# The first row stage of a Fourier and mixer kernel: second fold moved into the matmuls, small steps moved between engines, order of loads and scales changed

## The chip, the cores and the metric

The kernel runs on one core of a Trainium2 chip. The core's engines each work through a queue of their own in order: TensorE (PE in the profile; PEld is its loading of stationary operands), VectorE (DVE), ScalarE (ACT), GpSimd (POOL), and SyncE (SP), which here only issues DMAs. The metric is the device time of one execution in microseconds (us); lower is better.

## What is computed

Two operations are applied in turn, twice. The first adds to x the inverse transform of a filtered two-dimensional Fourier transform of its layernorm; the second is a token-mixing MLP. x has 2048 rows of 640 numbers, in float32.

```python
def _A_ref(x, w_r, w_i):
    X = rfft2(x)
    X = X * (w_r + 1j * w_i)
    return irfft2(X, s=(2048, 640))

x = x + _A_ref(_layernorm(x), w_r, w_i)
x = x + mixer_mlp(_layernorm(x), w1, b1, w2, b2)
x = x + _A_ref(_layernorm(x), w_r, w_i)
x = x + mixer_mlp(_layernorm(x), w1, b1, w2, b2)
```

## The kernel before

The 2048 rows lie in 16 tiles of 128 partitions by 640 columns, called row tiles 0 to 15 here. The whole program is written by hand as straight-line code; inside the stages spoken of here each engine executes its instructions in the order in which they are written (`self.pin`).

**The first row stage** (in `run`, a loop over steps i) takes each row tile through these steps, one step of the loop apart or so:

- SP loads the tile `xt` and, every fourth tile, a transform table `tM`. Further loads bring the sixteen filter tiles `w`.
- DVE takes the row statistics (`stats1`: two BATCH_NORM_STATS2, tile `st`; `stats2`: one BATCH_NORM_AGGREGATE, tile `mv`).
- ACT makes `nm` = -mean and `v` = variance + eps; POOL makes `r` = v to the power -1/2 and `nb` = nm times r; ACT makes the normalized tile `z`.
- First fold (`a0_fold1`): symmetric columns are added and subtracted by POOL, two TENSOR_TENSOR of 320 columns and a COPY of two columns, into `eo` (two buffers). POOL also sets two columns of `z` to zero.
- Second fold (`a0_fold2`): DVE adds and subtracts the halves of `eo` into `f` (two buffers): two instructions of 256 columns, two of 64 and a COPY.
- PE (`a0_s1f`): first `FILL` = 7 matmuls on constant data, which are no part of the result, then five float32 products of 128 columns each of `f` with the tile's table, into one of four PSUM tiles (`ps`).
- ACT and DVE evict the sums as a float16 pair: `s1h` (ACT) and `s1l` (DVE).

Beside these runs a scan: ACT squares every filter tile `w` with an accumulator (`jw`), from which a power-of-two scale `sx` for the filtered spectrum is found (`scale_x`); `scale_b` does the like for a bias. After the scans the first five tiles of `w` are fetched again (`self.wx`, `wfetch`) for the next stage.

**The next stage** (`a1`) follows a list of steps, `STEPS`. `d0`, `d1`, ... are PE's products along the columns; `d0` needs `s1h` and `s1l` of all sixteen row tiles. `ea1` to `ev9` are parts of `scale_b` and `scale_x`. From `d2` on, one operand, `stk`, is a part of `s1h` and `s1l` that was written to DRAM (`rest`) and read back in another layout. `sA0`, `sB0` and so on are PE's next products, `ph`, `pl`, `ta`, `tb` evictions and filtering by ACT and DVE.

Of the kernel before, what the change touches and what calls it, by code (L numbers as in the profile page):

```python
# [24 lines left out]
NW = 5  # L25
NSTK = 3
WARM = 4
FILL = 7
STEPS = '''
    ea1 ev1 ep8 ep1 ev8 ev2 d1@1 ep9 ev9 sA0@2 ph1 pl1 sB0 d2@3 sA1@0 d3@1 ph2&1 tb0 ta0 pl2 sa0 ph3 sB1 sb0 sA2@2 d4@3  # L30
    tb1 xh0&2 pl3 sB2 sA3@1 ta1 ph4&3 tb2 ta2 xl0 d6@0 sa1 sb1 ph6 sB3 xh1 d5@2 pl4 sa2 ta3 pl6 sb2 sA4@3 ph5 tb3 ul0&4
# [61 lines left out]
class Layers:  # L93
# [160 lines left out]
    def scan_x(self, pool, g):  # L254

        w = self.t(pool, [128, 2, NL], F32, "w", 3)
        self.nc.sync.dma_start(w, self.A["w"][g])
        junk = self.t(pool, [128, 2, NL], BF16, "jw", 1)
        return lambda: self.T.activation(junk, w, AF.Square, accum_out=self.xq[:, g:g + 1])

    def scale_x(self, pool, ps):

        V, mm = self.V, self.PE.matmul
        mm(ps[:NG, 0, 322:450], self.xq, self.eye, start=True, stop=True)
        yield
        m = pool.tile([NG, 1], F32, name="xm")
        V.tensor_reduce(m, ps[:NG, 0, 322:450], op=ALU.max, axis=mybir.AxisListType.X)
        b = pool.tile([NG, 128], F32, name="xb")
        V.tensor_copy(b, m.to_broadcast([NG, 128]))
        yield  # L270
        mm(ps[:, 1, 322:322 + NG], b, self.eye[:NG, :NG], start=True, stop=True)
        yield
        q = pool.tile([128, NG], F32, name="xqq")
        V.tensor_scalar(q, ps[:, 1, 322:322 + NG], SMALL, XS ** -2, op0=ALU.max, op1=ALU.mult)
        i = self.t(self.base, [128, NG], F32, f"qi{NG}", 1)
        a, b = i.bitcast(I32), self.sx.bitcast(I32)
        V.tensor_scalar(a, q.bitcast(I32), EXPO, 1, op0=ALU.bitwise_xor, op1=ALU.logical_shift_right)
        V.tensor_scalar(b, a, EXPO, None, op0=ALU.bitwise_and)
        V.tensor_scalar(self.sx, self.sx, 2.0 ** 63, None, op0=ALU.mult)
        yield  # L280
        V.tensor_scalar(a, b, EXPO, None, op0=ALU.bitwise_xor)
        V.tensor_scalar(q, i, EC * 0.5 / TS, None, op0=ALU.mult)
        of = pool.tile([128, NG], F32, name="xof")
        V.tensor_reduce(of, self.eye.rearrange("p (g a) -> p g a", g=NG), op=ALU.add, axis=mybir.AxisListType.X)
        V.tensor_tensor(of, of, q, op=ALU.mult)
        V.tensor_reduce(self.cxe, of, op=ALU.add, axis=mybir.AxisListType.X)
        yield
# [32 lines left out]
    def a0_open(self, first=False):  # L320
# [12 lines left out]
        if first:  # L333
            self.tM = [p.tile([128, 4, 128], F32, name=f"tM{q}_{self.n}") for q in range(4)]
        else:
            self.tM = [p.tile([128, 4, 2, 128], F16, name=f"tM{q}_{self.n}") for q in range(4)]
            self.tM32 = p.tile([128, 128], F32, name=f"tMf{self.n}")
# [37 lines left out]
    def a0_fold2(self, eo, between=lambda: None, gp=False):  # L375
# [6 lines left out]
        ea, eb = eb[:, :, 0:160], eb[:, :, 161:321]  # L382
        V.tensor_tensor(f4[:, 0::3], ea[:, :, :128], eb[:, :, :128], op=ALU.add)
        V.tensor_tensor(f5[:, 0::3], ea[:, :, 128:], eb[:, :, 128:], op=ALU.add)
        between()
        W.tensor_tensor(f4[:, 1:3], ea[:, :, :128], eb[:, :, :128], op=ALU.subtract)
        W.tensor_tensor(f5[:, 1:3], ea[:, :, 128:], eb[:, :, 128:], op=ALU.subtract)
# [19 lines left out]

    def a0_s1f(self, j, f):
        ps = self.big().rearrange("p a b -> p (a b)")
        for _ in range(FILL if j else 4 * FILL):  # L410
            self.PE.matmul(ps[:, :512], self.fill[:, :128], self.fill[:, 128:], start=True, stop=True)
        for t in range(5):
            c = slice(t * 128, t * 128 + 128)
            self.PE.matmul(ps[:, c], f[:, c], self.tM[j // 4][:, j % 4], start=True, stop=True)
        return ps[:, :D].rearrange("p (a h b) -> p a h b", h=2, b=4)
# [9 lines left out]
    def a0_tail(self, j, z, st, pend):  # L425
# [26 lines left out]
        for i, (c, w) in enumerate(((slice(0, 128), 512), (slice(128, 160), 128))):  # L452
            f = self.t(p, [128, w], F32, f"ft{i}", 1)
            f4 = f.rearrange("p (c b) -> p c b", c=4)
            V.tensor_tensor(f4[:, 0::3], ea[:, :, c], eb[:, :, c], op=ALU.add)
            V.tensor_tensor(f4[:, 1:3], ea[:, :, c], eb[:, :, c], op=ALU.subtract)
            if i:
# [25 lines left out]
    def a1(self, first):  # L483
# [268 lines left out]
        def scale(op):  # L752

            n = int(op[2:])
            if n > 7:
                if n == 8 and op[1] == "p":
                    made["x"] = self.scale_x(p, slots[3])
                next(made["x"])
            elif op == "ea1":
                made["b"] = self.scale_b(at=lambda: slots[3][:, 1, 400:401])  # L760
                next(made["b"])
            elif op in ("ev1", "ep1", "ev2"):
                next(made["b"])
            elif op in ("ea2", "ea3"):
# [1235 lines left out]
    def run(self):  # L2000
# [10 lines left out]
        self.eye = self.base.tile([128, 128], F32, name="eye")  # L2011
        scans = []
        x, st, z, eo, f, pv, vs, nms = ({} for _ in range(8))

        def load(i):
            if i < NJ:
                x[i] = self.t(self.pT, [128, D], F32, "xt", 6)
                self.lastld = nc.sync.dma_start(x[i], self.xs[0][i])
                if i % 4 == 0:
                    nc.sync.dma_start(self.tM[i // 4], A["tM32"][:, i:i + 4])  # L2020

        for i in range(3):
            load(i)
        self.pin = True
        for i in range(NJ + 6):
            load(i + 3)
            has = [0 <= i - k < NJ for k in range(7)]
            if has[6]:
                self.a0_s1h(i - 6, pv[i - 6], 1.0)
            if has[1]:  # L2030
                vs[i - 1] = self.t(self.pT, [128, 1], F32, "v", 2)
                nms[i - 1] = self.t(self.pT, [128, 1], F32, "nm", 2)
                self.T.activation(nms[i - 1], st[i - 1][:, 0:1], AF.Copy, scale=-1.0)
                self.T.activation(vs[i - 1], st[i - 1][:, 1:2], AF.Identity, bias=self.eps)
            if has[5]:
                pv[i - 5] = self.a0_s1f(i - 5, f.pop(i - 5))
            if has[3]:
                eo[i - 3] = self.a0_fold1(z.pop(i - 3))
            if has[2]:
                z[i - 2] = self.a0_norm(x.pop(i - 2), *st.pop(i - 2))  # L2040
            if has[0]:
                s1 = self.stats1(self.pT, x[i])
            if has[4]:
                s2 = []
                f[i - 4] = self.a0_fold2(eo.pop(i - 4), lambda: has[0] and s2.append(self.stats2(self.pT, s1)))
            elif has[0]:
                s2 = [self.stats2(self.pT, s1)]
            if has[0]:
                st[i] = s2[0]
            for k in () if i == 18 else (i - 7, i - 6) if i == 19 else (i - 6,):  # L2050
                if 0 <= k < NJ:
                    self.a0_s1l(k, pv.pop(k), 1.0)
            if has[1]:
                mv = st[i - 1]
                r = self.t(self.pT, [128, 1], F32, "r", 2)
                self.G.tensor_tensor(r, vs.pop(i - 1), self.mh, op=ALU.pow)
                b = self.t(self.pT, [128, 1], F32, "nb", 2)
                self.G.tensor_tensor(b, nms.pop(i - 1), r, op=ALU.mult)
                st[i - 1] = r, b
            if 4 <= i < NG + 4:  # L2060
                scans.append(self.scan_x(pw, i - 4))
            for _ in range(2 if i in (18, 19) else 1):
                if i >= 6 and scans:
                    scans.pop(0)()
# [232 lines left out]
```

## Time and profile before

| | us |
|---|---|
| median of 3 runs | 957.31 (956.43 to 957.54) |
| the profiled execution, its own time | 956.78 |
| its span, first to last instruction | 955.0 |

The profile is of that one execution; the 1.78 us by which its time exceeds its span lie around the instructions. Nearly all vector, scalar and GpSimd instructions go through one helper and carry its line, L85, so that groups are told apart by their tiles: `f<-eo` is an instruction that reads `eo` and writes `f`. "x2 [0.17 <-DVE f]" says that the row holds two instructions, that the engine was idle for 0.17 us before the first, and that an instruction of DVE on `f` ended the wait. In a row that groups several instructions, the duration runs from the first start to the last end. The row stage takes about the first 61 us of the span.

### The profile page before, as it was taken

To read this page: it belongs to the slowest core of one execution; us is meant where nothing else is said; L and a number is where in the kernel's file an instruction comes from. 1 tells how busy PE (TensorE), PEld (TensorE's weight loads), DVE (VectorE), ACT (ScalarE), POOL (GpSimd) and SP (SyncE) were. 2 spreads that over 40 slices of the span, in tenths; PEclk is the share of its full clock that TensorE was granted. 3 is DMA by queue.
4 is the path that set the end of the run, shared out by engine and by line. 5 is a ranking of instruction groups with operands and counts; after the bars stand their busy time and mean duration, and the time that the engine had idled before them with its cause. 6 is when DMAs were issued, how large, how long until landed. Compare 5 with 4: busy or idle time off the path is not lost.

```text
span 955.0 us, 22612 instructions
## 1 busy us (share of the span) xinstructions
PE 939.0 (98%) x9086; PEld 686.8 (72%) x9086; DVE 767.9 (80%) x1411; ACT 572.6 (60%) x889; POOL 301.1 (32%) x483
## 2 busy tenths in 40 slices
PE   8999999999999999999999999999999999999998
PEld 4667777767777777777777777777777777777776
DVE  7979999999888968877775898889745456998885
ACT  5857969895767665555543476884533335455542
POOL 6939968311111113332223596770000000000000
PEclk9999999999999999999999999999999999999999
DMA  7956367743886756755333655874554446555411
GB/s 252 310 174 193 103 205 239 244 177 138 302 309 233 254 197 232 259 187 178 115 118 119 174 167 168 264 242 157 159 170 158 150 129 238 190 185 186 142 55 48
DMA packets 69537, 179.50 MB, mean 188 GB/s; under 512 B 7836, under 2 KB 16312, under 8 KB 69432
## 3 DMA queue, kind: packets, MB, share of 16 engines
q1 hardware_dynamic: 62760, 153.94, 50.1%
q0 software_dynamic: 6672, 24.12, 6.6%
q8 instruction: 71, 1.16, 0.5%
q14 instruction: 34, 0.28, 0.1%
HBM read 130.45 MB, written 47.58 MB: 186 GB/s over the span
## 4 chain that ended last, share of the span: by engine, by line
PE 81%; DVE 9%; DMA 3%; ACT 2%; issue 2%; POOL 2%; SPq 1%; POOLq 0%; ACTq 0%; DVEq 0%
PE ps L85 81%; DVE st L85 1%; DMA raw<-w 1%; DVE f L85 1%; DVE s1l L85 1%; DVE Yl L85 1%; DVE xt L85 1%; DVE hl L85 1%; DVE hf L85 1%; DVE hlb L85 1%; POOL eo L85 1%; DMA xt<-x 1%; POOL xt L85 0%; DMA rest<-s1l 0%; ACT eh L85 0%
## 5 line engine op out<-in xcount | busy, mean ns | idle before, releaser
L85 PEld LDWEIGHTS <-wh 128*128 128x128 f16 x2290 | 221.9, 98 | 85.9 <-ACT wh L85 0.4
L85 PE MATMUL ps<-u,wh 128*128 128x320 f16 x1234 | 227.2, 299 | 0.0
L85 PEld LDWEIGHTS <-wl 128*128 128x128 f16 x1617 | 157.8, 98 | 62.1 <-issue 0.7
L85 PE MATMUL ps<-u,wl 128*128 128x320 f16 x817 | 180.7, 299 | 0.0
L85 PEld LDWEIGHTS <-wo 128*128 128x128 f16 x917 | 89.7, 98 | 34.8
L85 POOL TENSOR_TENSOR r<-v,mh 128x1 f32<-128x1 f32 x64 | 38.5, 601 | 123.3 <-DVE nm L85 113.7
L85 PE MATMUL ps<-tDi,Yh 128*128 128x322 f16 x320 | 69.9, 300 | 0.9 <-ACT Yh L85 0.8
L85 ACT ACTIVATE junk<-raw 128x896 bf16<-128x896 f32 (+1 forms) x60 | 59.5, 992 | 9.2 <-DMA raw<-w 8.1
L85 DVE SCALAR_TENSOR_TENSOR wl<-raw,s,wh 128x896 f16<-128x896 f32 (+2 forms) x43 | 55.7, 1304 | 11.3 <-ACT wh L85 11.3
L85 POOL TENSOR_TENSOR eo<-z 128x320 f32<-128x320 f32 x60 | 57.2, 974 | 18.6 <-ACT z L85 14.5
L85 POOL TENSOR_TENSOR xt<-xt,ec 128x320 f32<-128x320 f32 x64 | 53.3, 854 | 25.9 <-DVE xt L85 25.8
L85 DVE BATCH_NORM_STATS2 st<-xt 128x6 f32<-128x320 f32 x126 | 55.3, 480 | 4.9 <-DMA xt<-x 4.1
L85 PE MATMUL ps<-u,wo 128*128 128x320 f16 x413 | 57.9, 299 | 0.0
L85 PE MATMUL ps<-tDi,Yl 128*128 128x322 f16 x192 | 54.2, 299 | 0.1
L85 ACT ACTIVATE wh<-raw,s 128x896 f16<-128x896 f32 (+2 forms) x46 | 45.1, 988 | 6.1 <-PE ps L85 6.1
L85 POOL TENSOR_TENSOR xl<-ta,xh 128x642 f16<-128x642 f32 (+2 forms) x34 | 45.6, 1345 | 5.2 <-ACT xh L85 4.2
L85 DVE SCALAR_TENSOR_TENSOR u<-f,su,u 128x1280 f16<-128x1280 f32 (+2 forms) x26 | 25.5, 997 | 25.2 <-ACT u L85 25.1
L85 PE MATMUL ps<-hhb,wh 128*128 128x320 f16 x256 | 43.4, 299 | 0.0
L85 DVE TENSOR_TENSOR f<-eo 128x256 f32<-128x256 f32 x124 | 39.0, 367 | 5.0 <-POOL eo L85 3.5
L85 ACT ACTIVATE z<-xt,nb,r 128x640 f32<-128x640 f32 x31 | 28.5, 919 | 23.8 <-POOL z L85 15.9
L85 PE MATMUL ps<-tD,s1h 128*64 128x160 f16 (+1 forms) x576 | 39.3, 236 | 1.3 <-DVE Yl L85 0.7
L85 PEld LDWEIGHTS <-Yh 128*128 128x128 f16 x320 | 28.7, 97 | 14.4 <-ACT Yh L85 1.2
(262 smaller groups left out, 2217.3 us busy)
## 6 DMA issues: line engine op xcount, KB each, us to landing
xt<-x SPq DMA_DIRECT2D x79, 320.0 KB, 3.2
raw<-w SPq DMA_DIRECT2D x32, 512.0 KB, 7.0
w<-w SPq DMA_DIRECT2D x48, 321.0 KB, 3.4
x<-xt SPq DMA_DIRECT2D x47, 320.0 KB, 2.8
raw<-w SPq DMA_DIRECT2D x32, 448.0 KB, 5.2
raw<-w2z SPq DMA_DIRECT2D x32, 448.0 KB, 4.2
out<-xt SPq DMA_DIRECT2D x15, 320.0 KB, 2.2
w1S<-wl POOLq DMA_DIRECT2D x9, 512.0 KB, 6.1
```

Source lines behind the costliest of these rows:

```text
L85: i = f(*a, **k)
```

## The change

- In the first row stage the second fold is no longer done by DVE for the 128 main columns of each half. `eo` itself is the stationary operand, and PE multiplies it with the table and then with the table followed by its negative, summing in PSUM: four float32 products of 256 columns each take the place of four of 128. Only the last 32 columns of each half are still folded by DVE (`a0_rest`, tile `fr`). ACT makes the negative tables, one instruction per four row tiles.
- `eo` has three buffers, and its two odd columns are copied by DVE. The zero columns of `z` are set once.
- DVE adds eps to the variance; POOL's `nb` comes from one TENSOR_SCALAR on `mv`; ACT's `nm` and `v` go.
- The loads start with row tiles 0 and 1, then the table, then row tile 2. The filter tiles are scanned in the order 5 to 15, 0 to 4, and the last five stay for the next stage. The other tables load at step 13 in place of 8.
- `scale_b` and all of `scale_x` but its end run inside the loop and right behind it; their steps leave the head of `STEPS`.
- `FILL` is 1. The loop has 21 steps in place of 22.
- The order of the column groups changes, so `a0_fold2`, `a0_tail` and `dstage`, which the second layer uses too, index them in another order.

```diff
-FILL = 7
+FILL = 1
...
-    ea1 ev1 ep8 ep1 ev8 ev2 d1@1 ep9 ev9 sA0@2 ph1 pl1 sB0 d2@3 sA1@0 d3@1 ph2&1 tb0 ta0 pl2 sa0 ph3 sB1 sb0 sA2@2 d4@3
+    d1@1 sA0@2 ph1 pl1 sB0 d2@3 sA1@0 d3@1 ph2&1 tb0 ta0 pl2 sa0 ph3 sB1 sb0 sA2@2 d4@3
...
     def scan_x(self, pool, g):
 
-        w = self.t(pool, [128, 2, NL], F32, "w", 3)
-        self.nc.sync.dma_start(w, self.A["w"][g])
+        if g < NW:
+            w = self.wx[g] = self.wfetch(g)
+        else:
+            w = self.t(pool, [128, 2, NL], F32, "w", 4)
+            self.nc.sync.dma_start(w, self.A["w"][g])
         junk = self.t(pool, [128, 2, NL], BF16, "jw", 1)
...
         return ps[:, :D].rearrange("p (a h b) -> p a h b", h=2, b=4)
 
-    def a0_s1f(self, j, f):
+    def a0_fold0(self, z):
+
+        G, V = self.G, self.V
+        eo = self.t(self.pT, [128, 646], F32, "eo", 3)
+        v2 = lambda a, o, w: a[:, o:o + 2 * w].rearrange("p (a b) -> p a b", a=2)[:, :, 0:160]
+        za, zb = v2(z, 1, 161), v2(z, 321, 160)
+        V.tensor_copy(eo[:, 0:162:161], z[:, 0:162:161])
+        G.tensor_tensor(v2(eo, 1, 161), za, zb, op=ALU.add)
+        self.lastpool = G.tensor_tensor(v2(eo, 322, 161), za, zb, op=ALU.subtract)
+        return eo
+
+    def a0_rest(self, eo):
+
+        V = self.V
+        f = self.t(self.pT, [128, 128], F32, "fr", 2)
+        f4 = f.rearrange("p (c b) -> p c b", c=4)
+        eb = eo[:, 0:644].rearrange("p (a b) -> p a b", a=2)
+        ea, eb = eb[:, :, 128:160], eb[:, :, 289:321]
+        V.tensor_tensor(f4[:, 0::3], ea, eb, op=ALU.add)
+        V.tensor_tensor(f4[:, 1:3], ea, eb, op=ALU.subtract)
+        V.tensor_copy(f[:, 95:128:32], eo[:, 160:482:321])
+        return f
+
+    def a0_s1f(self, j, eo, f):
+
+        mm = self.PE.matmul
         ps = self.big().rearrange("p a b -> p (a b)")
-        for _ in range(FILL if j else 4 * FILL):
-            self.PE.matmul(ps[:, :512], self.fill[:, :128], self.fill[:, 128:], start=True, stop=True)
-        for t in range(5):
-            c = slice(t * 128, t * 128 + 128)
-            self.PE.matmul(ps[:, c], f[:, c], self.tM[j // 4][:, j % 4], start=True, stop=True)
+        for _ in range(FILL if j else 28):
+            mm(ps[:, :512], self.fill[:, :128], self.fill[:, 128:], start=True, stop=True)
+        m = self.tM[j // 4][:, :, j % 4]
+        eb = eo[:, 0:644].rearrange("p (a b) -> p a b", a=2)
+        for a in range(2):
+            o = ps[:, a * 256:a * 256 + 256].rearrange("p (c b) -> p c b", c=2)
+            mm(o, eb[:, a, :128], m[:, 0:1].to_broadcast([128, 2, 128]), start=True, stop=False)
+            mm(o, eb[:, a, 161:289], m, start=False, stop=True)
+        mm(ps[:, 512:640], f, m[:, 0], start=True, stop=True)
         return ps[:, :D].rearrange("p (a h b) -> p a h b", h=2, b=4)
 
...
-                terms = prods(part(c), table(2 * c))
+                terms = prods(part((0, 1, 3, 2)[c]), table(2 * c))
...
+        order = list(range(NW, NG)) + list(range(NW))
+        x, st, eo, fr, pv, rb = ({} for _ in range(6))
+        z = [self.pT.tile([128, 642], F32, name=f"z{k}") for k in range(2)]
+        for q in z:
+            nc.gpsimd.memset(q[:, D:], 0.0)
...
+        def table(q):
+            nc.sync.dma_start(self.tM[q][:, 0], A["tM32"][:, 4 * q:4 * q + 4])
+
+        load(0)
+        load(1)
+        table(0)
+        load(2)
         self.pin = True
-        for i in range(NJ + 6):
+        for i in range(NJ + 5):
+            has = [0 <= i - k < NJ for k in range(6)]
             load(i + 3)
...
+            if i in (4, 8, 12):
+                table(i // 4)
+            for _ in range(2 if i == 5 else 1):
+                if i >= 2 and order:
+                    scans.append(self.scan_x(pw, order.pop(0)))
...
-                with self.after(self.lastpool, self.lastld):
+            if i == 13:
+                with self.after(self.lastpool):
                     self.a0_load()
-        self.wx = {g: self.wfetch(g) for g in range(NW)}
-        for a in scans:
-            a()
+            if has[3]:
+                eo[i - 3] = self.a0_fold0(z[(i - 3) % 2])
+            if has[1]:
+                v, mv = st.pop(i - 1)
+                r = self.t(self.pT, [128, 1], F32, "r", 2)
+                self.G.tensor_tensor(r, v, self.mh, op=ALU.pow)
+                b = self.t(self.pT, [128, 1], F32, "nb", 2)
+                self.G.tensor_scalar(b, mv[:, 0:1], r, -1.0, op0=ALU.mult, op1=ALU.mult)
+                rb[i - 1] = r, b
+            if has[2]:
+                r, b = rb.pop(i - 2)
+                self.T.activation(z[i % 2][:, :D], x.pop(i - 2), AF.Identity, scale=r, bias=b)
+            if i % 4 == 2 and i < NJ:
+                q = self.tM[i // 4]
+                self.T.activation(q[:, 1], q[:, 0], AF.Copy, scale=-1.0)
+            for _ in range(2 if i == 7 else 1):
+                if i >= 4 and scans:
+                    scans.pop(0)()
+            if has[4]:
+                self.a0_s1h(i - 4, pv[i - 4], 1.0)
+            if i == 14:
+                gb = self.scale_b(at=lambda: px[:, 1, 400:401])
+            if i in (14, 15):
+                next(gb)
+            if has[0]:
+                s1 = self.stats1(self.pT, x[i])
+                mv = self.stats2(self.pT, s1)
+                v = self.t(self.pT, [128, 1], F32, "v", 2)
+                self.V.tensor_scalar(v, mv[:, 1:2], EPS, None, op0=ALU.add)
+                st[i] = v, mv
+            if i == NJ + 3:
+                next(self.gx)
+            if has[5]:
+                self.a0_s1l(i - 5, pv.pop(i - 5), 1.0)
+            if i == NJ + 2:
+                assert not scans
+                px = self.big()
+                self.gx = self.scale_x(self.pT, px)
+                next(self.gx)
+            if has[3]:
+                fr = self.a0_rest(eo[i - 3])
+                pv[i - 3] = self.a0_s1f(i - 3, eo.pop(i - 3), fr)
+            if i == NJ + 3:
+                next(self.gx)
+                next(gb)
+        next(self.gx)
+        next(gb)
```

More of the change, by code (lines that the diff above doesn't have):

```diff
@@ L265, in scale_x @@
         yield
-        m = pool.tile([NG, 1], F32, name="xm")
+        m = self.t(pool, [NG, 1], F32, "xm", 1)
         V.tensor_reduce(m, ps[:NG, 0, 322:450], op=ALU.max, axis=mybir.AxisListType.X)
-        b = pool.tile([NG, 128], F32, name="xb")
+        b = self.t(pool, [NG, 128], F32, "xb", 1)
         V.tensor_copy(b, m.to_broadcast([NG, 128]))
@@ L272, in scale_x @@
         yield
-        q = pool.tile([128, NG], F32, name="xqq")
+        q = self.base.tile([128, NG], F32, name="xqq")
         V.tensor_scalar(q, ps[:, 1, 322:322 + NG], SMALL, XS ** -2, op0=ALU.max, op1=ALU.mult)
@@ L282, in scale_x @@
         V.tensor_scalar(q, i, EC * 0.5 / TS, None, op0=ALU.mult)
-        of = pool.tile([128, NG], F32, name="xof")
+        of = self.base.tile([128, NG], F32, name="xof")
         V.tensor_reduce(of, self.eye.rearrange("p (g a) -> p g a", g=NG), op=ALU.add, axis=mybir.AxisListType.X)
@@ L333, in a0_open @@
         if first:
-            self.tM = [p.tile([128, 4, 128], F32, name=f"tM{q}_{self.n}") for q in range(4)]
+            self.tM = [p.tile([128, 2, 4, 128], F32, name=f"tM{q}_{self.n}") for q in range(4)]
         else:
@@ L382, in a0_fold2 @@
         ea, eb = eb[:, :, 0:160], eb[:, :, 161:321]
-        V.tensor_tensor(f4[:, 0::3], ea[:, :, :128], eb[:, :, :128], op=ALU.add)
+        V.tensor_tensor(f4[:, 0::2], ea[:, :, :128], eb[:, :, :128], op=ALU.add)
         V.tensor_tensor(f5[:, 0::3], ea[:, :, 128:], eb[:, :, 128:], op=ALU.add)
         between()
-        W.tensor_tensor(f4[:, 1:3], ea[:, :, :128], eb[:, :, :128], op=ALU.subtract)
+        W.tensor_tensor(f4[:, 1::2], ea[:, :, :128], eb[:, :, :128], op=ALU.subtract)
         W.tensor_tensor(f5[:, 1:3], ea[:, :, 128:], eb[:, :, 128:], op=ALU.subtract)
@@ L454, in a0_tail @@
             f4 = f.rearrange("p (c b) -> p c b", c=4)
-            V.tensor_tensor(f4[:, 0::3], ea[:, :, c], eb[:, :, c], op=ALU.add)
-            V.tensor_tensor(f4[:, 1:3], ea[:, :, c], eb[:, :, c], op=ALU.subtract)
+            plus, minus = (slice(0, 4, 3), slice(1, 3)) if i else (slice(0, 4, 2), slice(1, 4, 2))
+            V.tensor_tensor(f4[:, plus], ea[:, :, c], eb[:, :, c], op=ALU.add)
+            V.tensor_tensor(f4[:, minus], ea[:, :, c], eb[:, :, c], op=ALU.subtract)
             if i:
@@ L465, in a0_tail @@
             q = (self.big() if i else warm)[:, 0, :n]
-            for o in (0,) if i else (0, 384, 128, 256):
+            for o in (0,) if i else (0, 256, 128, 384):
                 self.PE.matmul(q[:, o:o + 128], f[:, o:o + 128], mr, start=True, stop=True)
@@ L755, in scale @@
             if n > 7:
[L756 to L763, printed above, removed]
+                next(self.gx)
             elif op in ("ea2", "ea3"):
@@ L2011, in run @@
         self.eye = self.base.tile([128, 128], F32, name="eye")
-        scans = []
-        x, st, z, eo, f, pv, vs, nms = ({} for _ in range(8))
+        scans, self.wx = [], {}
+        order = list(range(NW, NG)) + list(range(NW))
[3 more added lines that the diff above has]
+            nc.gpsimd.memset(q[:, D:], 0.0)
         def load(i):
@@ L2017, in load @@
                 x[i] = self.t(self.pT, [128, D], F32, "xt", 6)
[L2018 to L2023, printed above, removed]
+                nc.sync.dma_start(x[i], self.xs[0][i])
+        def table(q):
[3 more added lines that the diff above has]
+        table(0)
@@ L2024, in run @@
+        load(2)
         self.pin = True
-        for i in range(NJ + 6):
+        for i in range(NJ + 5):
+            has = [0 <= i - k < NJ for k in range(6)]
             load(i + 3)
[L2027 to L2064, printed above, removed]
@@ L2068, in run @@
                 nc.sync.dma_start(self.b2, self.A["b2"])
-                with self.after(self.lastpool, self.lastld):
+            if i == 13:
+                with self.after(self.lastpool):
                     self.a0_load()
-        self.wx = {g: self.wfetch(g) for g in range(NW)}
-        for a in scans:
-            a()
+            if has[3]:
[43 more added lines that the diff above has]
+                next(gb)
+        next(self.gx)
+        next(gb)
         self.pin = False
```

## The prediction

> **What bounds the kernel now.** I read the page first, then the chain of waits over the first 95 us, then the timeline and the groups by shape of the same stretch.
>
> ```profile
> span 955.0 us, 22612 instructions
> PE 939.0 (98%) x9086; PEld 686.8 (72%) x9086; DVE 767.9 (80%) x1411; ACT 572.6 (60%) x889; POOL 301.1 (32%) x483
> 26.00:46.00 20.00, 19.68 (x115) 12.59 (x116) 19.79 (x59) 16.89 (x40) 18.41 (x40) 1.00 0.93 321
> ```
>
> The page calls PE busy for 98% of the span, but in the row stage that is no bound: the third row (a view by windows: PE, PEld, DVE, ACT, POOL busy, granted clock, DMA share, GB/s) has PE, DVE and POOL nearly full at once, and 7 of PE's 17 instructions for a row tile are fills. The chain says what really sets the pace:
>
> ```profile
> 38.22 0.82 DVE s1l L85
> 39.04 0.79 DVE st L85 x2
> 39.83 0.06 DVE f L85
> 39.89 0.47 issue
> 40.36 0.21 DVE f L85
> 40.57 0.12 DVE mv L85
> 40.69 0.44 DVE f L85 x2
> ```
>
> ```profile
> 38.46 1.70 POOL L85 TENSOR_TENSOR eo<-z 128x320 f32<-128x320 f32 x2 [0.17 <-DVE f L85]
> 39.75 0.82 DVE L85 TENSOR_TENSOR f<-eo 128x256 f32<-128x256 f32 x2
> 41.46 1.69 POOL L85 TENSOR_TENSOR eo<-z 128x320 f32<-128x320 f32 x2 [0.18 <-DVE f L85]
> ```
>
> One row tile takes 41.46 - 38.46 = 3.00 us, and the timeline shows a ring: POOL's two folds (1.70) end at 40.16; DVE's first `f`, issued at 39.75, gets on only then (the 0.47 of "issue"); four more instructions on `f` and the statistics follow; and POOL's next fold starts only when DVE has let go of the `eo` buffer ("0.17 <-DVE f"). With two buffers, neither engine can be ahead of the other. Four marks bound the stage; the first two are folds of row tiles 0 and 15:
>
> ```profile
> 9.41 1.69 POOL L85 TENSOR_TENSOR eo<-z 128x320 f32<-128x320 f32 x2
> 53.18 1.88 POOL L85 TENSOR_TENSOR eo<-z 128x320 f32<-128x320 f32 x2 [0.77 <-DVE f L85]
> 60.09 0.82 DVE L85 SCALAR_TENSOR_TENSOR s1l<-ps,s1h 128x640 f16<-128x640 f32 x1 [0.59 <-ACT s1h L85]
> 68.22 0.46 PE L85 MATMUL ps<-tD,stk 96*64 96x160 f16 x8
> ```
>
> So: fold 0 at 9.41, fold 15 at 53.18 (43.77 later), the last `s1l` done at 60.91 (7.73), `d2` with its first `stk` product at 68.22 (7.31).
>
> **The change, part by part.** *The pace.* Durations of what remains (groups of 25.7 to 46.7 us; the last three rows are by tile over the whole run, in ns: min/median/max):
>
> ```profile
> L85 POOL TENSOR_TENSOR eo<-z 128x320 f32<-128x320 f32 x14 | 11.9, 868 | 1.0 <-DVE f L85 1.0
> L85 DVE TENSOR_TENSOR f<-eo 128x64 f32<-128x64 f32 x14 | 3.0, 212 | 0.0
> L85 ACT ACTIVATE z<-xt,nb,r 128x640 f32<-128x640 f32 x7 | 6.4, 919 | 1.3 <-POOL nb L85 1.2
> L85 ACT ACTIVATE s1h<-ps 128x640 f16<-128x640 f32 x8 | 5.5, 683 | 0.0
> L85 ACT ACTIVATE jw<-w 128x642 bf16<-128x642 f32 x7 | 5.1, 727 | 1.4 <-DMA w<-w 1.4
> L85 POOL TENSOR_TENSOR r<-v,mh x64: 537/548/1307, 5.3 to 644.1; 128x1 f32<-128x1 f32 x64
> L85 DVE TENSOR_SCALAR v<-mv x48: 153/153/155, 130.8 to 643.9; 128x1 f32<-128x1 f32 x48
> L85 POOL TENSOR_SCALAR nb<-mv,r x30: 264/264/267, 131.7 to 643.3; 128x1 f32<-128x1 f32 x30
> ```
>
> - POOL per row tile: two folds 1.69, `r` 0.55, the new `nb` 0.26 (this very form is used later): 2.50. The COPY and the MEMSET go.
> - DVE: the two instructions of 256 columns go; two of 64 stay (0.42), `st` 0.79, `mv` 0.21, `s1l` 0.82, two COPYs (0.17 each, below), and `v` 0.15 comes: 2.73 end to end. The chain shows 0.12 for `mv` and 0.44 for a 256 and a 64 together, so neighbours overlap by 0.05 to 0.1; I take 2.5.
> - ACT loses `nm` and `v`: `z` 0.92, `jw` 0.73 and its accumulator's read 0.19, `s1h` 0.68 make 2.52 end to end. The negative table, 512 columns once in four row tiles, is not in the trace: between 0 (overlapped) and 0.73 (`jw`, 642 columns), so at most 0.18 per row tile. All of it hides behind POOL, with a step to spare each way, since `z` is needed a step later.
> - PE:
>
> ```profile
> 38.69 0.50 PE L85 MATMUL ps<-tM,f 128*128 128x128 f32 x3
> 38.80 0.39 PE L85 MATMUL ps<-tM,f 128*128 128x128 f32 x2
> 42.02 1.67 PE L85 MATMUL ps<-fill 128*128 128x512 f16 x7
> ```
>
> One more float32 instruction adds 0.50 - 0.39 = 0.11, and a product is two of them. 256 columns are not in the trace: between 0.11 (cost all in the weights) and 0.22 (all in the columns) each. I take 0.22: 8 x 0.22, 2 x 0.11 and one fill (1.67/7 = 0.24) are 2.2 us. That hides.
>
> POOL is then the slowest, and with three buffers it waits for no DVE instruction of the same row tile. I take 2.6 us per row tile: 2.50 and 0.1 for hand-overs and meetings with DVE; bounds 2.45 and 2.9 (DVE's 2.73 without overlap and one meeting).
>
> The meetings are what may spoil it:
>
> ```profile
> 12.23 1.69 POOL L85 TENSOR_TENSOR eo<-z 128x320 f32<-128x320 f32 x2
> 12.40 0.72 DVE L85 COPY f<-eo 128x2 f32<-128x2 f32 x1
> 38.14 0.17 DVE L85 COPY f<-eo 128x2 f32<-128x2 f32 x1
> 20.79 1.78 DVE L85 TENSOR_TENSOR f<-eo 128x256 f32<-128x256 f32 x2
> ```
>
> A COPY of two columns takes 0.17 alone and 0.72 when POOL is inside a fold, and two instructions on `f` (0.50 alone) took 1.78 at 20.79. In the changed loop the four DVE instructions that can be so held (two on `fr`, two COPYs) stand one behind the other, 0.6 us in all, right behind the end of POOL's second fold, while POOL is on `r` and `nb` (0.8 us). They fit, and a DVE that comes early is held just until that fold ends, which puts it back in this place. "SBUF — State Buffer" of the Trainium skill (Who interferes with whom) says that GpSimd and a DVE COPY or TENSOR_SCALAR can exclude each other for a whole instruction. The COPYs agree; for the new `v`, which falls into POOL's folds, that rule would add up to 0.87 a row tile, but 48 of them here took 153 to 155 ns, none longer, so I add nothing.
>
> *From fold 0 to fold 15:* 14 steps of 2.6, then one of 1.68 (row tile 15 has no `r` and `nb` behind it): 38.1 in place of 43.77. **Saves 5.7.**
>
> *The start.* DVE takes row tile 0 when it lands, then waits for 1:
>
> ```profile
> 3.69 0.89 DVE L85 BATCH_NORM_STATS2 st<-xt 128x6 f32<-128x320 f32 x2 [1.95 <-DMA xt<-x]
> 6.97 0.89 DVE L85 BATCH_NORM_STATS2 st<-xt 128x6 f32<-128x320 f32 x2 [2.16 <-DMA xt<-x]
> ```
>
> Between lie a table of 256 KB and the tile of 320 KB: 3.28 us for 576 KB. Without the table in between, 256/576 of it, 1.46, goes; bounds 0 and 1.46, and I take 1.3. The chain from there to fold 0 is as long as before. Row tile 2 still has the table ahead. **Saves 1.3.**
>
> *The end.* Before, 7.73. After: two folds and one meeting 1.95, DVE's rest of row tile 14 (held by them) 0.2, PE's product on it 0.3, the product for `scale_x` that now stands ahead in PE's queue 0.25, fill and nine products 2.4, `s1h` 0.70, `s1l` 0.85: 6.65. That `scale_x` product waits for the last `jw` on ACT, with row tile 15's products queued behind it; the last `w` should be there. **Saves 1.1.** Filter tiles are no longer fetched twice: 1.6 MB less on SP's queue.
>
> *The head of the next stage.* `scale_b` and `scale_x` stood in PE's way between `d0`, whose last products are the first row here, and `d1`, the second. But `d2` waits for `stk`:
>
> ```profile
> 61.27 0.72 PE L85 MATMUL ps<-tD,s1l 128*64 128x160 f16 x16
> 63.39 0.33 PE L85 MATMUL ps<-tD,s1h 128*64 128x160 f16 x4
> 60.94 0.33 SPq L547 DMA_DIRECT2D rest<-s1l  x1
> 64.90 0.68 SPq L533 DMA_DIRECT2D stk<-rest  x1
> DMA to landing us min/median/max: 2.8/2.8/2.8
> ```
>
> From 61.99 to 63.39 PE lost 1.4, which would go. But `s1l` is written to DRAM at 60.94, its read-back issued at 64.90 and landed at 67.7 (last row: of that DMA), 0.5 before PE used it at 68.22. This follows the last `s1l`, whatever PE does. So of 1.4 at most 0.5 is kept, and I take 0.25; PE is late at `stk` next. **Saves 0.25.** From there on the list of steps and PE's load are the same, and PE carries the chain from 77 us, so the gain is handed on whole.
>
> Sum: 5.7 + 1.3 + 1.1 + 0.25 = 8.35. From the profiled execution's 956.78 that is 948.4; this lies 0.5 below the median of 957.31, so for a median I forecast **949.0**.
>
> **The rivals.** A measurement of this kernel can tell about 0.2%, 1.9 us, from no change.
>
> - *Slower: the ping-pong of 20.79 in every row tile.* If DVE's group slips behind POOL's next fold, its instructions and the folds alternate: 1.78 in place of 0.50, of which about 0.7 adds to the pace. At 3.3 us, 14 x 0.7 = 9.8 more: 958.8. It decides from a pace of 2.6 + 8.35/14 = 3.2. For it: DVE and POOL are only 0.1 apart. Against it: the place behind the fold is one DVE is put back into.
> - *The loads set the pace.* A row tile needs `xt` 320, `w` 321 and a quarter table 64 KB: 722 kB in 2.6 us is 278 GB/s; 321 were moved between 26 and 46 us. But the last `w` stands behind the other tables (1.6 MB): all 13.2 MB at 321 GB/s take 41 us, so it lands about when it is due, and at 295 some 3 us later: 952.
> - *The gain is lost later:* another load or wait in the next stage holds PE up for most of it: 956.
> - *PE's clock falls* with six of seven fills gone. At half the clock a row tile would take 4.4, slower by 25 us net of nothing else: about 974. The windows speak against it:
>
> ```profile
> 20.00:22.00 2.00, 1.34 (x7) 0.68 (x6) 2.00 (x6) 1.77 (x5) 1.92 (x4) 1.00 0.89 295
> ```
>
> PE was busy for 1.34 of 2.00 at a granted clock of 1.00; I expect 2.2 of 2.6. "TensorE: Matmul & The Clock Gate" of the Trainium skill (Part 1) halves the clock after an idle window of about 3.4 us; by it too, gaps of 0.4 would not.
>
> **How the numbers follow.** Forecast (pace 2.45 to 2.9) 0.70; loads 0.13, also faster; lost later 0.06, same; ping-pong 0.08 and clock 0.03, slower. Low end: pace 2.45 (-2.1), all of the 1.46 and the 0.5 (-0.4), a shorter end by a meeting fewer (-1.0): 945.5. High end: pace 2.9 (+4.2), which covers the loads: 953.2. Faster 0.83, same 0.06, slower 0.11.
>
> **What would show it.** Folds of neighbouring row tiles 2.6 apart on POOL, with no wait on DVE; COPYs near 0.17, not 0.7; fold 0 near 8.1; the last `s1l` done near 52.8; PE idle ahead of `stk`, about 1 us; the clock at 1.00. I am wrong if POOL's folds are over 3 us apart, if ACT waits for `w` by microseconds, or if the gain at `d2` is not that at the end.

## The result and the profile after

The changed kernel takes 948.03 us (median of 4 runs, 947.56 to 948.93), the kernel before 956.89 beside it (4 runs, 956.43 to 957.54): a ratio of 0.9907, with a 95% interval of 0.9895 to 0.992. The forecast was 949.0, in a range of 945.5 to 953.2. The profiled span fell from 955.0 to 946.6, by 8.4; the sum of the forecast was 8.35. Its terms came out quite otherwise:

| from, to | before | after | saved | forecast |
|---|---|---|---|---|
| span's start to fold 0 | 9.41 | 9.96 | -0.55 | 1.3 |
| fold 0 to fold 15 | 43.77 | 39.11 | 4.66 | 5.7 |
| fold 15 to the last `s1l` done | 7.73 | 4.83 | 2.90 | 1.1 |
| last `s1l` done to the first `stk` product | 7.31 | 5.85 | 1.46 | 0.25 |
| sum | 68.22 | 59.75 | 8.47 | 8.35 |

The page and the view by windows of the changed kernel:

```profile
span 946.6 us, 22342 instructions
PE 932.1 (98%) x8996; PEld 685.5 (72%) x8996; DVE 753.9 (80%) x1411; ACT 569.0 (60%) x861; POOL 296.8 (31%) x453
```

```profile
20.00:22.00 2.00, 1.88 (x11) 1.29 (x10) 1.79 (x5) 1.97 (x5) 2.00 (x4) 1.00 0.77 229
```

Columns as before: PE, PEld, DVE, ACT and POOL busy, granted clock, DMA share, GB/s. PE is still "98% busy", which says as little as before; the granted clock is 1.00 here, and now PE, DVE, ACT and POOL are all busy for 1.79 to 2.00 of these 2.00 us. The loop's pace, in the timeline of POOL and then of DVE of the changed kernel (start, duration, engine, line, operation, tiles):

```profile
27.94 1.70 POOL L85 TENSOR_TENSOR eo<-z 128x320 f32<-128x320 f32 x2
29.60 0.55 POOL L85 TENSOR_TENSOR r<-v,mh 128x1 f32<-128x1 f32 x1
30.24 0.26 POOL L85 TENSOR_SCALAR nb<-mv,r 128x1 f32<-128x1 f32 x1
30.50 1.70 POOL L85 TENSOR_TENSOR eo<-z 128x320 f32<-128x320 f32 x2
```

```profile
27.63 0.16 DVE L85 COPY eo<-z 128x2 f32<-128x2 f32 x1
...
29.00 0.81 DVE L85 SCALAR_TENSOR_TENSOR s1l<-ps,s1h 128x640 f16<-128x640 f32 x1
29.73 0.35 DVE L85 TENSOR_TENSOR fr<-eo 128x64 f32<-128x64 f32 x2
30.11 0.17 DVE L85 COPY fr<-eo 128x2 f32<-128x2 f32 x1
30.19 0.16 DVE L85 COPY eo<-z 128x2 f32<-128x2 f32 x1
```

A row tile takes 30.50 - 27.94 = 2.56 us on POOL and 30.19 - 27.63 = 2.56 on DVE, and neither has a wait in it (one step, from 20.10 to 22.83, took 2.73 with a wait of 0.17 for DVE). The `fr` pair starts at 29.73, behind the end of POOL's second fold (27.94 + 1.70 = 29.64), and both COPYs take 0.17 or less: the place that the prediction gave them.

Two places cost more. The start (timeline of the changed kernel, all engines):

```profile
4.84 0.88 DVE L85 BATCH_NORM_STATS2 st<-xt 128x6 f32<-128x320 f32 x2
...
5.95 0.92 ACT L85 ACTIVATE z<-xt,nb,r 128x640 f32<-128x640 f32 x1 [1.02 <-POOL nb L85]
...
8.40 0.89 DVE L85 BATCH_NORM_STATS2 st<-xt 128x6 f32<-128x320 f32 x2 [2.26 <-DMA xt<-x]
...
9.71 0.16 DVE L85 COPY eo<-z 128x2 f32<-128x2 f32 x1
...
9.96 1.70 POOL L85 TENSOR_TENSOR eo<-z 128x320 f32<-128x320 f32 x2 [2.81 <-DVE eo L85]
```

`z` of row tile 0 is ready at 5.95 + 0.92 = 6.87. Fold 0 waits until 9.96, not for `z` but for DVE's COPY of two columns into the same `eo`; the COPY stands in DVE's queue behind the statistics of row tile 2, and those wait for a load that is behind the table. The statistics of row tile 1 come at 4.84, 2.13 earlier than the 6.97 before; but from there to fold 0 it takes 5.12 in place of 2.44. Before, the COPY was POOL's own and stood behind the folds.

And steps 13 to 15 (timelines of POOL, DVE and ACT of the changed kernel):

```profile
40.73 1.70 POOL L85 TENSOR_TENSOR eo<-z 128x320 f32<-128x320 f32 x2
...
44.06 1.69 POOL L85 TENSOR_TENSOR eo<-z 128x320 f32<-128x320 f32 x2 [0.75 <-DVE eo L85]
...
49.07 1.69 POOL L85 TENSOR_TENSOR eo<-z 128x320 f32<-128x320 f32 x2 [0.81 <-DVE eo L85]
```

```profile
41.19 0.16 DVE L85 TENSOR_REDUCE sqb<-sqs 128x1 bf16<-128x1 f32 x1 [0.61 <-ACT bsq L85]
```

```profile
39.04 0.61 ACT L85 ACTIVATE tM<-tM 128x512 f32<-128x512 f32 x1
39.56 0.72 ACT L85 ACTIVATE jw<-w 128x642 bf16<-128x642 f32 x1
...
40.87 0.20 ACT L85 ACTIVATE bsq<-b1s 128x14 f32<-128x14 f32 x1
```

`scale_b`'s reduction on DVE waits for ACT, where its square is queued behind the negative table, a filter tile and an eviction (`s1h`, 40.28 to 40.96). DVE has no slack, so the fold behind it comes 3.33 after the one before (40.73 to 44.06), 0.77 over the pace. The last fold waits 0.81 because it has no `r` and `nb` ahead of it to hide DVE's `fr` and COPYs.

The end and the head, in the timelines of DVE and PE of the changed kernel:

```profile
53.08 0.82 DVE L85 SCALAR_TENSOR_TENSOR s1l<-ps,s1h 128x640 f16<-128x640 f32 x1 [0.56 <-ACT s1h L85]
```

```profile
50.20 1.89 PE L85 MATMUL ps<-tM,eo 128*128 128x256 f32 x8
...
59.68 0.24 PE L85 MATMUL ps<-tD,s1l 128*64 128x161 f16 x2
59.75 0.45 PE L85 MATMUL ps<-tD,stk 96*64 96x160 f16 x8
```

PE begins the products of row tile 15 at 50.20, while POOL's second fold still runs to 49.07 + 1.69 = 50.76: the first half of `eo` needs only the first fold. And PE comes to `stk` without a wait, from a product on `s1l`.

### The profile page after: what moved, and what is told of

Its sections match the earlier page's. It is cut to its first block, busy times and chain, and to the rows that moved or that the text cites. A ratio compares the mean times of both kernels' runs of the same rounds, so it can differ in the third digit from the quotient of the medians.

```text
span 946.6 us, 22342 instructions
## 1 busy us (share of the span) xinstructions
PE 932.1 (98%) x8996; PEld 685.5 (72%) x8996; DVE 753.9 (80%) x1411; ACT 569.0 (60%) x861; POOL 296.8 (31%) x453
## 4 chain that ended last, share of the span: by engine, by line
PE 81%; DVE 9%; POOL 3%; ACT 3%; DMA 2%; issue 2%; SPq 0%; DVEq 0%; ACTq 0%; POOLq 0%
PE ps L85 81%; DVE st L85 2%; DMA xt<-x 1%; POOL xl L85 1%; DVE s1l L85 1%; DMA raw<-w 1%; POOL ta L85 1%; DVE xt L85 1%; POOL eo L85 1%; DVE hl L85 1%; DVE hf L85 1%; DVE hlb L85 1%; DVE fr L85 1%; POOL xt L85 0%; ACT eh L85 0%
## 5 line engine op out<-in xcount | busy, mean ns | idle before, releaser
L85 DVE SCALAR_TENSOR_TENSOR f<-ps,cp,f 128x320 f32<-128x320 f32 x41 | 22.4, 545 | 19.7 <-PE ps L85 19.7
```

The lines of the kernel that those rows point to most:

```text
L85: i = f(*a, **k)
```

## Theories and experiments

The theory after the result: DVE's queue, full at 2.56 us per row tile, sets the pace with POOL just below; the gain of the loop comes from the fold that DVE lost; the start and `scale_b` each cost something that the change need not pay. The rivals are the prediction's own reasons: a ring through too few `eo` buffers, POOL as the slowest engine, a head bounded by the read-back of `stk`. Below, "before" is the median of the kernel before in the same set of runs, and the interval is of the ratio to it.

### A third buffer alone, in the kernel before

Three buffers in the first row stage, two behind it:

```diff
-        eo = self.t(self.pT, [128, 646], F32, "eo", 2)
+        eo = self.t(self.pT, [128, 646], F32, "eo", self.neo)
...
+        self.neo = 3
...
+        self.neo = 2
```

> The kernel before with a third eo buffer in the first row stage and nothing else. Theory (the ring broke because the second fold left DVE and the small steps left POOL): the third buffer alone frees little, since POOL's own steps for a row tile last 1.69 + 0.38 + 0.10 + 0.54 + 0.19 = 2.9 us end to end with meetings; pace 2.75 to 2.95 in place of 3.00, time 1 to 4 us below before (953 to 956). Rival (the third buffer is what breaks the ring): pace near 2.6, time near 951.

Measured: 956.33 against 956.95, ratio 0.9996 (0.9986 to 1.0005): no change, less even than the theory allowed. The timelines of POOL, DVE and PE of this kernel:

```profile
28.99 1.70 POOL L85 TENSOR_TENSOR eo<-z 128x320 f32<-128x320 f32 x2
...
31.77 1.69 POOL L85 TENSOR_TENSOR eo<-z 128x320 f32<-128x320 f32 x2
```

```profile
49.54 2.75 DVE L85 TENSOR_TENSOR f<-eo 128x256 f32<-128x256 f32 x4
```

```profile
53.10 0.49 PE L85 MATMUL ps<-tM,f 128*128 128x128 f32 x2 [0.64 <-DVE f L85]
53.42 1.67 PE L85 MATMUL ps<-fill 128*128 128x512 f16 x7
...
56.05 1.67 PE L85 MATMUL ps<-fill 128*128 128x512 f16 x7
```

The folds do run ahead: 31.77 - 28.99 = 2.78 apart in place of 3.00. But the gain does not reach the end of the stage: fold 15 comes 1.88 earlier than before (51.30), the last `s1l` is done only 0.47 earlier (60.44). Four instructions on `f`, which took 1.01 and 1.03 for the next two row tiles, took 2.75 at 49.54, inside POOL's last folds; this is the ping-pong that the prediction feared for the changed kernel. So PE still waits for DVE's `f` at 53.10, and from there, with seven fills, it needs 56.05 - 53.42 = 2.63 for each row tile that is left. So two buffers did cost the loop some 0.2 per row tile, and giving a third alone is worth nothing. In these 2.78 POOL waits for nobody: two folds, COPY, MEMSET, `r` and `nb` follow each other, the COPY with 0.39 here and 0.18 further on (48.09). No run of the changed kernel puts the COPY and the MEMSET back on POOL by themselves, so how the gain divides between them and the fold that left DVE is not shown.

### Two buffers in the changed kernel

```diff
-        eo = self.t(self.pT, [128, 646], F32, "eo", 3)
+        eo = self.t(self.pT, [128, 646], F32, "eo", 2)
```

> The changed kernel with two eo buffers again. Theory: DVE and PE have let go of a buffer long before POOL's next but one fold needs it, pace 2.56 as with three, time 948 within 1 us. Rival (the third buffer carries the gain): pace 2.8 or more, POOL waits on fr or PE ahead of eo, time 951.5 or more.

Measured: 948.70 against 956.95, ratio 0.9919 (0.9905 to 0.9934), which cannot be told from the changed kernel's 0.9907. Its folds in POOL's timeline:

```profile
29.43 1.71 POOL L85 TENSOR_TENSOR eo<-z 128x320 f32<-128x320 f32 x2
...
32.01 1.72 POOL L85 TENSOR_TENSOR eo<-z 128x320 f32<-128x320 f32 x2
```

They are 2.58 apart and wait for nobody. The third buffer is no part of the gain.

### The second fold back on DVE

`a0_s1v` is PE's part of the kernel before, five products of 128 columns, with `FILL` 1; the negative tables go.

```diff
-                fr = self.a0_rest(eo[i - 3])
-                pv[i - 3] = self.a0_s1f(i - 3, eo.pop(i - 3), fr)
+                f = self.a0_fold2(eo.pop(i - 3))
+                pv[i - 3] = self.a0_s1v(i - 3, f)
```

> The changed kernel with the second fold back on DVE (two instructions of 256 columns more, five products of 128 columns, no negative tables), all else kept. Theory: DVE is the pace setter at 2.56 and gets 0.6 to 0.7 more a row tile, so pace 3.1 to 3.3 and 14 x 0.6 = 8 to 10 us more: 956 to 958. Rival (POOL's lighter load and the buffers gave the gain): pace 2.8 or less, time 951 or less.

Measured: 957.82, ratio 1.001 (1.0001 to 1.002): the whole gain is gone. POOL's and DVE's timelines of this kernel:

```profile
28.46 1.71 POOL L85 TENSOR_TENSOR eo<-z 128x320 f32<-128x320 f32 x2 [0.31 <-DVE eo L85]
...
30.78 0.60 POOL L85 TENSOR_SCALAR nb<-mv,r 128x1 f32<-128x1 f32 x1
31.69 1.68 POOL L85 TENSOR_TENSOR eo<-z 128x320 f32<-128x320 f32 x2 [0.31 <-DVE eo L85]
```

```profile
30.31 1.02 DVE L85 TENSOR_TENSOR f<-eo 128x256 f32<-128x256 f32 x4
```

The four fold instructions take 1.02 in place of `fr`'s 0.35, and a row tile takes 31.69 - 28.46 = 3.23, more than the 3.00 before, for DVE now has `v` and the COPY too; POOL waits 0.31 for it each time. The moves of small steps to DVE pay only because the second fold leaves it. In this kernel POOL's `nb` takes 0.60 beside DVE's folds, 0.26 in the changed one. "SBUF — State Buffer" of the Trainium skill (Who interferes with whom) says that a DVE instruction with two SBUF inputs contends with a GpSimd instruction that reads SBUF; this row agrees.

### Seven fills

```diff
-FILL = 1
+FILL = 7
```

> The changed kernel with seven fills in place of one in front of a row tile's products. Theory: PE needs 2.2 a row tile and six more fills of 0.215 make it 3.5, so PE sets the pace at 3.5 and the time is 14 x 0.94 = 13 us more: 961. Rival (the fills fall into PE's idle time as they did before): pace 2.6 to 2.8, time 948 to 951.

Measured: 961.78, ratio 1.0058 (1.0041 to 1.0074). The view by windows of this kernel:

```profile
30.00:40.00 10.00, 10.00 (x51) 7.32 (x49) 7.29 (x27) 7.05 (x13) 6.99 (x13) 1.00 1.00 369
```

The time is what the theory gave (961). PE is full, 10.00 of 10, and folds come 3.46 apart (3.5 forecast); DVE, ACT and POOL are busy for some 7 of it. Dropping the fills is a condition of the change; the granted clock of 1.00 with one fill shows that they were not needed for it here.

### DVE and POOL each a little longer

Three more `v` on DVE in each row tile, and in another kernel one more `nb` on POOL, all unread:

```diff
+                for q in range(3):
+                    u = self.t(self.pT, [128, 1], F32, f"u{q}", 2)
+                    self.V.tensor_scalar(u, mv[:, 1:2], EPS, None, op0=ALU.add)
```

> Three more of the one-element v instructions on DVE in each row tile, whose results nobody reads. Independent small instructions start about 0.07 apart on DVE (COPY fr at 27.55, COPY eo at 27.63 after the change), so DVE gets some 0.2 more per row tile. Theory (after the change DVE and POOL are both full at 2.56): each row tile takes 2.75, 15 of them add 3: 951. Rival (as predicted: POOL is the pace, DVE has 0.1 to spare): at most 0.1 per row tile, 948 to 949.5.

```diff
+                u = self.t(self.pT, [128, 1], F32, "nb2", 2)
+                self.G.tensor_scalar(u, mv[:, 0:1], r, -1.0, op0=ALU.mult, op1=ALU.mult)
```

> One more nb instruction on POOL in each row tile, whose result nobody reads: 0.26 more per row tile. Theory (POOL and DVE both full at 2.56): 2.8 per row tile, 15 of them add 3.9: 952. Rival (the chain of waits is right to run through DVE and POOL has slack): less than 0.1 per row tile, 948 to 949.5.

Measured: 949.23 (948.11 to 949.89) and 950.40 (949.93 to 952.02) against 956.69, ratios 0.9918 (0.9906 to 0.9929) and 0.9934 (0.9921 to 0.9946). POOL's timeline, with three more `v` and then with one more `nb`:

```profile
28.67 1.69 POOL L85 TENSOR_TENSOR eo<-z 128x320 f32<-128x320 f32 x2 [0.17 <-DVE eo L85]
...
31.41 1.69 POOL L85 TENSOR_TENSOR eo<-z 128x320 f32<-128x320 f32 x2 [0.17 <-DVE eo L85]
```

```profile
28.63 1.70 POOL L85 TENSOR_TENSOR eo<-z 128x320 f32<-128x320 f32 x2
...
30.93 0.50 POOL L85 TENSOR_SCALAR nb<-mv,r 128x1 f32<-128x1 f32 x2
31.39 1.69 POOL L85 TENSOR_TENSOR eo<-z 128x320 f32<-128x320 f32 x2
```

With 0.18 more on DVE a row tile takes 2.74 and POOL waits for DVE in each: DVE was full. With 0.24 more on POOL it takes 2.76, without a wait: POOL was nearly full too. So on the pace both theories (2.75 and 2.8) came out: the two engines lie within some 0.05 of each other. A cut on either one alone would then gain little; that is argued from these rows, not run. The times came out 1.8 and 1.6 below the 951 and 952 of the theories, and 949.23 is even inside the rival's range: by time alone the run with three more `v` decides nothing, and it is POOL's wait in the trace that speaks for DVE. From fold 0 to fold 15 the two kernels take 40.81 and 41.23, against 39.11: 1.70 and 2.12 more. With three more `v` the first two steps and the last two keep a pace of 2.5, so the slower pace holds for fewer than 15 row tiles.

### The table behind row tile 2

```diff
         load(0)
         load(1)
-        table(0)
         load(2)
+        table(0)
```

> One line moved: the first quarter of the table is loaded behind row tile 2, not ahead of it. Theory (start): after the change row tile 2's statistics wait for their load until 8.40, DVE's two-column COPY for fold 0 is queued behind them, and so fold 0 starts at 9.96 although z of row tile 0 is ready at 6.87. Without the table ahead, row tile 2 lands by about 256/576 of 3.28, 1.4, earlier, fold 0 comes to 8.6 or 8.7, and the whole row stage is 1.2 to 1.4 earlier: 946.6 to 946.9. Rival (loads): the loads of the later row tiles (DMA share 0.94 from 10 to 20 us) then hold the loop back, or PE waits for the table: fold 0 earlier, but fold 15 at 49 as before, 948.0.

Measured: 947.49 (946.53 to 947.88) against 956.75, ratio 0.9902 (0.9888 to 0.9915). DVE's and POOL's timelines of this kernel:

```profile
6.23 0.88 DVE L85 BATCH_NORM_STATS2 st<-xt 128x6 f32<-128x320 f32 x2
...
7.53 0.16 DVE L85 COPY eo<-z 128x2 f32<-128x2 f32 x1
9.20 0.89 DVE L85 BATCH_NORM_STATS2 st<-xt 128x6 f32<-128x320 f32 x2 [1.52 <-DMA xt<-x]
```

```profile
7.77 1.72 POOL L85 TENSOR_TENSOR eo<-z 128x320 f32<-128x320 f32 x2 [0.46 <-DVE eo L85]
...
11.22 1.69 POOL L85 TENSOR_TENSOR eo<-z 128x320 f32<-128x320 f32 x2 [0.85 <-DVE eo L85]
```

Fold 0 comes at 7.77, before the 8.6 expected here and the 8.1 of the prediction: it was indeed held by the statistics of row tile 2 and the table ahead of its load. But half of the rival holds as well: row tile 3 is then late (9.20), and fold 1 comes at 11.22, only 1.26 before the changed kernel's 12.48. Even that is not all due to the edit: in nine traces with the table ahead, fold 0 comes between 9.01 and 10.24 and fold 1 between 11.54 and 12.77. The time lies between theory and rival, and by time alone this edit cannot be told from the changed kernel.

### `scale_b` two steps later

```diff
-            if i == 14:
+            if i == 16:
                 gb = self.scale_b(at=lambda: px[:, 1, 400:401])
-            if i in (14, 15):
+            if i in (16, 17):
```

> The first two steps of scale_b are called in steps 16 and 17 of the row loop, not 14 and 15. Theory: the one long pace after the change (3.33 in place of 2.56 between the 13th and 14th folds, 40.73 to 44.06) comes from DVE's square of scale_b, which waits 0.61 for its copy on ACT, behind the negative table, jw and s1h. Two steps later there is no negative table and hardly a jw on ACT, and DVE has no statistics: the 0.77 goes, fold 15 comes at 48.3 and the time is 947.3. Rival: the steps only meet the end of the stage in its place, where DVE's s1l set the end: last s1l as before (53.9) or later, 948.0 to 948.5.

Measured: 947.11 (945.93 to 947.31), ratio 0.9897 (0.9883 to 0.991). POOL's timeline at the place of the long step:

```profile
40.12 1.71 POOL L85 TENSOR_TENSOR eo<-z 128x320 f32<-128x320 f32 x2
...
42.68 1.70 POOL L85 TENSOR_TENSOR eo<-z 128x320 f32<-128x320 f32 x2
```

The step takes 2.56 again: `scale_b` was the cause of the 0.77. From fold 0 to fold 15 it is 38.38, 0.73 less than the 39.11 after the change, and in its new place `scale_b` holds nobody up (last `s1l` done 4.90 after fold 15, 4.83 after the change). Fold 15 comes at 47.70, not 48.3, because fold 0 came 0.64 earlier (9.32), which this edit does not explain.

### `scale_b` and `scale_x` back at the head of the next stage

```diff
-    d1@1 sA0@2 ph1 pl1 sB0 d2@3
+    ea1 ev1 ep8 ep1 ev8 ev2 d1@1 ep9 ev9 sA0@2 ph1 pl1 sB0 d2@3
...
-                next(self.gx)
+                if n == 8 and op[1] == "p":
+                    made["x"] = self.scale_x(p, slots[3])
+                next(made["x"])
+            elif op == "ea1":
+                made["b"] = self.scale_b(at=lambda: slots[3][:, 1, 400:401])
+                next(made["b"])
+            elif op in ("ev1", "ep1", "ev2"):
+                next(made["b"])
...
-            if i == 14:
-                gb = self.scale_b(at=lambda: px[:, 1, 400:401])
-            if i in (14, 15):
-                next(gb)
...
-                px = self.big()
-                self.gx = self.scale_x(self.pT, px)
-                next(self.gx)
```

> Only this part of the change is undone: scale_b and scale_x stand again at the head of the next stage's list, as before. Theory A (as in the prediction: stk's landing bounds the head, at most 0.5 is kept): between the last s1l and the first stk product 0.25 to 0.5 comes back, while the 0.77 that scale_b costs inside the row loop goes: 947.5 to 947.8. Theory B (after the trace: PE's own work sets this head, since the read-back landed 0.18 before PE used it after the change and 0.57 before it): the head is 1.4 longer again, less the 0.77 and some 0.2 at the stage's end: 948.4 to 948.7. They also differ in the write and read-back: by A the time from the write of s1l to the issue of its read-back (4.0 before, 2.9 after) is chance; by B it may go back to 4.0.

Measured: 948.46 (947.91 to 949.32), ratio 0.9913 (0.99 to 0.9927), as theory B has it. Theory A's 947.5 to 947.8 lies below all five runs, but not clear of the interval; the trace decides. PE's and SP's timelines of this kernel:

```profile
53.46 0.39 PE L85 MATMUL ps<-eye,xq 128*16 128x128 f32 x2
54.77 0.16 PE L85 MATMUL ps<-sqb,ones 128*128 128x1 bf16 x1 [0.92 <-DVE sqb L85]
54.86 0.33 PE L85 MATMUL ps<-tD,s1h 128*64 128x160 f16 x4
...
59.69 0.45 PE L85 MATMUL ps<-tD,stk 96*64 96x160 f16 x8
```

```profile
52.48 0.33 SPq L580 DMA_DIRECT2D rest<-s1l  x1
...
55.26 0.67 SPq L566 DMA_DIRECT2D stk<-rest  x1
```

Between `d0` and `d1` PE has only the two scale products and loses 1.4 (53.46 to 54.86), and the first `stk` product is 7.24 behind the last `s1l` (done at 52.45), 1.39 more than the 5.85 after the change. The read-back of `stk`, issued at 55.26 and 2.63 later in place, has by then been ready for 1.8. So PE's own queue sets the head, and taking the scales out of it is worth the whole 1.4.

### The two edits together

Both edits, the table behind row tile 2 and `scale_b` two steps later; then once more beside the changed kernel itself.

> The two edits together: the table behind row tile 2, and scale_b's first steps at 16 and 17. Theory: the two act at different places and add, 1.2 to 1.4 and 0.7: 945.9 to 946.2, faster than both kernels. Rival: with fold 15 some 2 earlier, the last loads of w or the loads of row tiles hold the loop instead and one of the two is lost: 946.8 to 947.5.

Measured: 946.83 (946.06 to 947.28) against 956.75, ratio 0.9896 (0.9882 to 0.9909). This misses the theory's 945.9 to 946.2 and lies at the near end of the rival's range.

> The changed kernel itself once more, beside the next run on the same chip, as the measure for it. Every theory: 947.6 to 948.3.

> The table behind row tile 2 and scale_b's first steps at 16 and 17 once more, to be compared with the changed kernel on the same chip. Theory: from the second fold on, the long pace of 0.77 is gone, and the second fold itself comes 0.3 to 1.2 earlier: 1.0 to 1.6 less than the changed kernel, 946.3 to 947.0. Rival: the landing of the first row tiles scatters by as much, and only the 0.77 shows: 947.2 to 947.5.

Measured on one chip: the changed kernel 948.23 (5 runs, 947.24 to 949.86), the two edits 947.07 (4 runs, 946.32 to 947.59). Over both sets the mean is 946.88 with the edits (8 runs) and 948.29 without (9 runs, those of the result among them), 1.4 less. The runs of the two kernels overlap only between 947.24 and 947.59, but the intervals of their ratios to the kernel before (0.9881 to 0.9909 and 0.9894 to 0.9923) overlap too. The 947.07 lies between the theory's range and the rival's. `scale_b` moved alone, above, is no slower than the two edits (947.11, mean 946.87 of 4 runs). So the times do not show that the table's move adds anything to it. In the traces fold 15 comes at 47.70 with `scale_b` alone and at 47.37 and 47.30 with both, and the first loads scatter by more than that.

## Why the prediction was right, and where it was not

- **"With two buffers, neither engine can be ahead of the other"** held for the kernel before only (2.78 with three), and the conclusion drawn from it, that the third buffer frees POOL, failed: the changed kernel keeps its pace with two. There `r` and `nb`, 0.8 us on POOL between the folds, cover DVE's hand-over (`fr` and the COPYs, 29.73 to 30.35).
- **"POOL is then the slowest"**, 2.6 from a sum of 2.50: the size was right (2.56), the engine not quite. DVE, estimated at 2.5, is full at 2.56; POOL needs only some 0.05 less (2.50 to 2.52 in the first and last steps, where DVE has fewer instructions). What made 2.6 right was that the second fold left DVE, as the run with the fold back on it shows; what the small steps that left POOL add to that was not tried by itself.
- **"From fold 0 to fold 15: saves 5.7"**; 4.66. The ordinary steps were 0.4 better than forecast in sum (30.77 for twelve, against 31.2). Two terms were left out: `scale_b`'s hold of 0.77 inside the loop (the prediction lets ACT's work hide behind POOL, but here DVE waited for ACT and had no slack), and the wait of 0.81 ahead of the last fold, which has no `r` and `nb` to hide it.
- **"The chain from there to fold 0 is as long as before"** is the step of the start that failed. The COPY moved from POOL's queue behind the folds to DVE's queue ahead of them, past the statistics of row tile 2. That chain, from row tile 1's statistics to fold 0, took 5.12 in place of 2.44. The earlier load itself brought more than the 1.3 (2.13), but fold 0 came 0.55 later in all. With the table one tile later fold 0 came at 7.77.
- **The end** was summed in series (6.65; measured 4.83): two folds, then all that follows. But row tile 14's `fr` and its products, the `scale_x` product and the fill (1.0 in the sum) are under way before POOL's second fold ends, and PE begins with the half of `eo` that the first fold has made, 0.56 before the second fold ends. The eight instructions of 256 columns took 1.89, 0.24 each, where 0.22 was taken.
- **The head: `stk`'s landing "follows the last `s1l`, whatever PE does"**, so at most 0.5 of 1.4 is kept, is the step of the head that failed. PE came to `stk` with no wait in all of these traces but the one with seven fills, and the whole 1.4 was kept. The row that misled was SP's: 4.0 from the write of `s1l` to the issue of its read-back, taken as a fixed length. After the change it was 2.9, and 2.8 with the scales back in the old place. PE was not idle ahead of `stk`, as the prediction had said it would be.
- **The sum** (8.35; 8.47 measured) was right by luck, because these errors cancel: 1.85 and 1.04 too much at the start and in the loop, 1.80 and 1.21 too little at the end and the head. The marks on the way were missed: fold 0 at 9.96, not near 8.1, and the last `s1l` done at 53.90, not near 52.8. What was right by its reasons is the pace of the loop. The gain was handed on whole (8.47 at `stk`, 8.4 in the span), as forecast.
- **The rivals:** no ping-pong was seen in the changed loop (COPYs 0.17), the granted clock was 0.999 or 1.000 in each run of it, and no gain was lost later. The loads do not set the pace of the middle, though they set the first two folds.
- **`v` adds nothing of its own.** By tile, over the changed kernel's whole run:

```profile
L85 DVE TENSOR_SCALAR v<-mv x64: 153/154/155, 4.8 to 635.6; 128x1 f32<-128x1 f32 x64
```

All 64 took 153 to 155 ns, those inside POOL's folds too; the added 0.87 by the rule weighed in the prediction did not come.

## What to carry to other kernels

Where several engines are nearly full at once, a step pays only if it is taken off the full engine and put where there is room, and what it needs beside it comes too: here the fold off DVE needed the fills off PE, and a third buffer by itself did nothing. Follow every small instruction that changes its queue to the first and the last pass of the loop, where the work that hides it is missing: a COPY of 0.16 us held fold 0 back by 3.1 us (9.96, with `z` ready at 6.87), and with the `fr` steps ahead of it fold 15 by 0.8. And before a transfer is called the bound of what follows, look whether the engine waits for it; here one that landed 0.5 ahead of its use had not been waited for.

## What was not expected of the hardware

- The landing of the first loads scatters. With the same order of loads, the statistics of row tile 2 began at 8.40 and 8.69 in two traces of the changed kernel, at 7.76 where only `scale_b` had moved and at 7.46 with two buffers; fold 0 follows, and a good part of the 1 to 2 us between runs of one kernel may be that.
- The time from the write of `s1l` to the issue of its read-back was 4.0 in the kernel before and 3.9 with a third buffer in it, and between 2.6 and 3.5 in the other traces, whose order of loads is the changed one. PE's order is not the reason (2.8 with the scales at the old place). What is, stays open. The second fetch of filter tiles in the kernel before was not tried by itself; it was over by then, for the DMA engines moved nothing from 58 to 60 us.
